# Narrow matrices on TensorE: where the transposes of maxima, the gate logits and V's scale matmul stand beside the P V bursts

## The chip, the cores and the metric

The kernel runs on one NeuronCore of a Trainium2 chip. The metric is the device time of one execution in microseconds (us). TensorE (PE) is shown in the profile as two rows: PE, the matmuls, and PEld, the loads of the stationary matrix that goes with each matmul. The other engines are VectorE (DVE), ScalarE (ACT), GpSimd (POOL) and SyncE (SP), which only issues DMAs here.

## The reference

An attention over 8 batches and 8 heads, and a mixture of experts behind it. Queries are averaged in pairs first, so that 576 pooled queries meet 1152 keys of 64 numbers each.

```python
q_pool = q.reshape(B, H, S // 2, 2, D).mean(axis=3)
scores = np.matmul(q_pool, k.transpose(0, 1, 3, 2)) / np.sqrt(D)
scores = scores - np.max(scores, axis=-1, keepdims=True)
attn = np.exp(scores)
attn = attn / (np.sum(attn, axis=-1, keepdims=True) + 1e-09)
attn_out = np.matmul(attn, v)
...
x = attn_out.transpose(0, 2, 1, 3).reshape(B * S, H * D)      # 4608 x 512
logits = x @ w_gate                                           # 8 experts
e_idx = np.argmax(logits, axis=1)
...
h = np.maximum(x[mask] @ w1[e], 0.0)
out[mask] = gate_w[mask, None] * eom[mask, e, None] * (h @ w2[e])
```

## The kernel before

**Stages.** First comes the attention, over 32 pairs of heads (8 batches of 4 pairs); it fills about the first two thirds of the span. Behind it stand the expert layers (`Moe.run`), which the change leaves alone. Nearly all matmuls of the attention are in one of two formats: fp32r (shown as f32 in the profile) for scores, maxima and logits, and f16 for P V.

**One step.** The attention runs in steps `s`, 18 for a pair, and the order on each engine is the order in which the Python loop emits (`manual_schedule`). One step emits on PE:

- the scores of one key chunk of one head, transposed (keys on partitions): two matmuls of L393 and two of L395, each with its own load of 128 columns, 288 columns wide. The exponentials on ACT (L399/L400 or L407/L408) follow, in two PSUM buffers that alternate;
- one chunk of row maxima in an even step and two in an odd one: two matmuls of L330 (384 columns wide), whose product DVE reduces to one maximum per query (L331). This runs 18 steps ahead of the scores that need it;
- in even steps only, a **P V burst** of the pair that is behind by `ALAG` = 6 steps: `BURST` says how many key chunks, mostly two. A chunk is 15 matmuls (L424, L425, L426) 64 or 65 columns wide, each with its own f16 load of 128 columns.

**The small work between.** Three kinds of small PE work stand among these, and they are what the change moves.

- *Transposes of maxima* (`rows`, L365): when the maxima of 4 or 5 query tiles are complete, the 128 x 4 or 128 x 5 tile `m` is transposed by a matmul whose stationary matrix is `m` itself (4 or 5 columns) and whose moving one is the identity, 128 columns wide. In the next step DVE splits the result in two parts `mr` (L370, L371), and in the step after that ACT issues two small DMAs (L125, `qb<-mr`) that put them as extra rows into `qb`, which the scores read. There are 64 of them; before the change 58 stood between L330 and a P V burst.
- *Gate logits* (`logits`, L496): when a pair's P V is normalised, its 128 columns of x are transposed (L479), split in high and low parts, and multiplied by the gate weights `wgt`: two matmuls, high and low, for 256 rows of x and two more for 320 rows. `wgt` has 32 columns that matter, padded with zeros to `WC` = 128. A generator yields 0 or 1 after each piece: the loop at `for r in routers` calls it at the head of a step, after a yield of 1 only in an even one. So the logits stood at the head of an even step, before its scores. There are 64 such pairs of matmuls.
- *V's scale* (`gmax`, L272): one fp32 matmul with a matrix of ones (128 columns loaded) and two columns moving; the profile shows it as two passes. The table `PREP` gives for each preparatory work of a pair the third of a step at which it is emitted: phase 0 is just behind the scores, phase 1 just behind the first chunk of maxima, phase 2 at the end of the step. `gmax` stood at 93, phase 0. There is one per pair.

`psum()` hands out three PSUM buffers in turn for L330, L365, L479, L496 and L272; some of these hold one until DVE has read it.

Of the kernel before, what the change touches and what calls it, by code (L numbers as in the profile page):

```python
# [26 lines left out]
         (45, 'sl', 0, 1), (46, 'sk', 1, 0), (48, 'sk', 1, 1), (51, 'sq1'), (54, 'sl', 1, 0), (57, 'sl', 1, 1), (56, 'lv'),  # L27
         (78, 'amax', 0), (82, 'amax', 1), (99, 'gmax'), (100, 'scale', 0), (100, 'scale', 1), (100, 'scale', 2), (103, 'vh', 0), (103, 'vs', 0), (106, 'vh', 1), (107, 'vl', 0), (109, 'vs', 1), (113, 'vl', 1))
PREP = ((0, 'lk'), (12, 'kh', 0), (12, 'qsum'), (17, 'kh', 1), (18, 'kl'), (18, 'dk', 0), (19, 'dk', 1), (22, 'qh'), (24, 'dq', 0), (25, 'dq', 1), (26, 'ql'), (29, 'qd'), (30, 'dl', 0), (32, 'dl', 1),
        (63, 'lv'), (82, 'amax', 0), (88, 'amax', 1), (93, 'gmax'), (94, 'scale', 0), (95, 'scale', 1), (99, 'scale', 2), (100, 'vh', 0), (101, 'vs', 0), (103, 'vl', 0), (107, 'vh', 1), (107, 'vs', 1), (110, 'vl', 1))  # L30
BURST = {0: 2, 2: 2, 4: 2, 6: 2, 8: 1, 10: 2, 12: 2, 14: 2, 16: 3}
PLP = (1, 3, 7, 9, 11, 13)
PLPL = (1, 3, 5, 17)
# [11 lines left out]
P32 = 6  # L45
SLEAD = 32
S = 1152
WC = 128
NQ = 576
NC = 9  # L50
SHIFT = 4.0 * math.log(2.0)
# [15 lines left out]
def attention(tc, qT, kT, vL, wg, keep, xrows, idscr, cum, pairs, setup, scat, init, exps):  # L67
    nc = tc.nc
    nb = len(pairs) // 4
    with ExitStack() as ctx:  # L70
# [16 lines left out]
        def psum(hold=False, name="tp"):  # L87

            while len(held) == 3:
                pop() if fill else pendv.pop(0)()  # L90
            k = next(i for i in banks if i not in held)
            free(k)
            if hold:
                held.add(k)
            x = ps_m.tile([128, 512], F32, name=name, tag=f"mp{k}")
            return (x, k) if hold else x

        def free(k):
            held.discard(k)
            banks.remove(k)  # L100
            banks.append(k)
# [22 lines left out]
        def dmaf(o, i, q=nc.sync):  # L124
            q.dma_start(out=o.bitcast(F32), in_=i.bitcast(F32))  # L125
# [220 lines left out]
        def pop(k=1):  # L346
            while k and fill:
                fill.pop(0)()
                k -= 1
# [3 lines left out]
        def sends():  # L353

            while pendd and pendd[0][1] < now[0]:
                pendd.pop(0)[0]()
# [3 lines left out]
        def rows(force=False):  # L360
            while pend_t and (force or now[0] >= pend_t[0][-1] + TLAG):
                m9, nt, t0, t1, qbf, _ = pend_t.pop(0)
                tp, tk = psum(True)
                tp = tp[0:nt, 0:128]
                nc.tensor.transpose(out=tp, in_=m9[:, 0:nt], identity=ident)  # L365
                mr = sm.tile([5, 2, 128], F32R, name="mr")[0:nt]
                c0 = 16.0 * SHIFT

                def split(tp=tp, tk=tk, mr=mr, qbf=qbf, t0=t0, t1=t1, nt=nt):
                    nc.vector.tensor_scalar(out=mr[:, 0], in0=tp, scalar1=c0, scalar2=None, op0=ALU.subtract)  # L370
                    nc.vector.scalar_tensor_tensor(out=mr[:, 1], in0=tp, scalar=c0, in1=mr.bitcast(F32)[:, 0], op0=ALU.subtract, op1=ALU.subtract)  # L371
                    free(tk)

                    def send():
                        for j in range(2):
                            dmaf(qbf[66 + j:67 + j, 128 * t0:128 * t1].rearrange("o (t n) -> o t n", n=128), mr[:, j], nc.scalar)
                    pendd.append((send, now[0]))
                if now[0] < 18:
                    split()
                else:  # L380
                    pendv.append(split)
# [60 lines left out]
        routers = []  # L442

        wf = bp.tile([128, 4, 16], F32, name="wf")
        wgt = bp.tile([128, 4, WC], F32R, name="wgt")
        em8 = keep['em8']
# [23 lines left out]
        def logits(b, c, xb):  # L470

            xh = sm.tile([128, NQ], F32R, name="xh", bufs=1)
            xl = sm.tile([128, NQ], F32R, name="xl", bufs=1)
            yield 1
            for c0, c1, grp in ((0, 256, (0, 1)), (256, NQ, (2, 3, 4))):
                tx, tk = psum(True)
                for i, t in enumerate(grp):
                    x = xb[:, t, 128 * c:128 * c + 128]
                    nc.tensor.transpose(out=tx[:, 128 * i:128 * i + 128], in_=x, identity=ident)  # L479
                d = 0  # L480
                for o, w in ((0, c1 - c0),) if c0 == 0 else ((0, 256), (320, 64)):
                    z = slice(c0 + d, c0 + d + w)
                    nc.scalar.copy(out=xh[:, z], in_=tx[:, o:o + w])

                    def sub(o=o, w=w, z=z, tx=tx, tk=tk if not d else None):
                        nc.vector.tensor_tensor(out=xl[:, z], in0=tx[:, o:o + w], in1=xh.bitcast(F32)[:, z], op=ALU.subtract)
                        if tk is not None:
                            free(tk)
                    fill.insert(0, sub)
                    d += w  # L490
                yield 1
            for c0, c1 in ((0, 256), (256, NQ)):
                pop(99)
                tl = psum()
                for j, x in enumerate((xh, xl)):
                    nc.tensor.matmul(tl[:, 0:c1 - c0], lhsT=wgt[:, c], rhs=x[:, c0:c1], start=j == 0, stop=j == 1)  # L496
                if c == 0:
                    nc.vector.tensor_copy(out=lT[:, c0:c1], in_=tl[0:32, 0:c1 - c0])
                else:
                    nc.vector.tensor_tensor(out=lT[:, c0:c1], in0=tl[0:32, 0:c1 - c0], in1=lT[:, c0:c1], op=ALU.add)  # L500
                yield 1
            if c == 3:
                yield from router(b, xb)

# [117 lines left out]
        def adv(k, g, want):  # L622
            while pos[k] < want:
                next(g, None)
                pos[k] += 1
# [3 lines left out]
        def prep_at(s, ph):  # L629
            u = 3 * (s + SLEAD) + ph  # L630
            for n in range(max(u // 54 - 2, 0), min(u // 54 + 2, NP)):
                r = u - 54 * n + min(3 * (LEAD - 15), 2 * n)
                if r == 0:
                    preps[n] = prep(n, PREP if n > 1 else PREP0 if n else PREPF)
                if n in preps:
                    for f in preps[n].pop(r, ()):
                        f()

        E = mybir.EngineType
        with tc.manual_schedule(engines={E.PE, E.DVE, E.Activation, E.Pool}):  # L640
            for s in range(-SLEAD, 0):
                for ph in range(3):
                    prep_at(s, ph)
                if s == -RI:
                    for i in (1, 2):
                        dmaf(QBs[i][64:66], QBs[0][64:66])
                        dmaf(KBs[i][64:68], KBs[0][64:68])
                if s == 1 - SLEAD + INIT:
                    consts()
                if s == -3:  # L650
                    init(0)
                if s >= -int(L0):
                    adv('m', mg, int(1.5 * (s + 1 + L0)))
                    now[0] = s
                    sends()
                    pop(3)
                    rows()
            for s in range(18 * NP + 14):
                now[0] = s
                live = s < 18 * NP  # L660
                if s % 18 == 2 and 0 < s // 18 < 5:
                    with tc.issue_after(lastk[0].ins):
                        init(s // 18)
                sends()
                while pendv:
                    pendv.pop(0)()
                for r in routers:
                    if not s % 2 or not live or not r[1]:
                        r[1] = next(r[0], 0)
                pop()  # L670
                if live:
                    next(sg)
                prep_at(s, 0)
                mw = min(27 * NP, int(1.5 * (s + 1 + min(LEAD, L0 + LS * s))))
                if pos['m'] < mw:
                    adv('m', mg, pos['m'] + 1)
                prep_at(s, 1)
                adv('m', mg, mw)
                if s < 54 or s % 2 == 0:
                    rows()  # L680
                if pos['m'] == 27 * NP:
                    pop(2)
                j = s - ALAG
                for _ in range(BURST.get(j % 18, 0) if 0 <= j < 18 * NP else 0):
                    next(ag)
                prep_at(s, 2)
                if not live:
                    pop(3)
            pop(99)
            for r in routers:  # L690
                for _ in r[0]: pass
# [513 lines left out]
```

## Time and profile before

| | before |
|---|---|
| time, median of 3 runs | 1521.67 us (1519.01 to 1526.12) |
| the profiled execution's own time | 1524.1 us |
| its span | 1522.4 us |
| PE busy, share of the span | 1477.5 us, 97% |
| PEld busy | 1339.5 us, 88% |
| DVE, ACT, POOL busy | 72%, 74%, 66% |
| granted TensorE clock, mean | 0.995 |

A row of the timeline reads: start in us from the span's start, duration in us, engine, line, operation, tiles (written <- read), shapes, and how many such instructions in a row were merged. Matmuls overlap in a pipeline, so the duration of one says little; what one costs is read from the distance between starts. Starts are shown to 0.01 us, and a distance worked out from two of them is good to about that much. A row of the groups reads: line, engine, operation, tiles, shapes, count, then busy time in us, mean duration of one in ns, and the idle time before it with what ended it.

### The profile page before, as it was taken

The page shows a single profiled execution, that of the slowest core. Times are in us where ns is not written, and L with a number is a line of the kernel's source. Part 1 is how long each engine was busy: PE and PEld are TensorE (multiplying, and loading weights), DVE is VectorE, ACT ScalarE, POOL GpSimd, SP SyncE. Part 2 cuts the span into 40 slices and gives each one's busy share as a digit, 9 for nine tenths or more (in the row PEclk, how much of TensorE's full clock was granted, in tenths as well). Part 3 has the DMA queues.
Part 4 walks back from the last instruction along what each step waited for, and adds up shares of the span by engine and source line. Part 5 has one row for each costly group of instructions (what it writes and reads, how often), then busy time and mean ns, then how long its engine had stood idle before and what let it go on. Part 6 is the DMA issues. An engine that isn't in the chain of part 4 may idle for free. (4 is left out here: it accounts for less than half of the span.)

```text
span 1522.4 us, 40889 instructions
## 1 busy us (share of the span) xinstructions
PE 1477.5 (97%) x15838; PEld 1339.5 (88%) x15838; DVE 1103.0 (72%) x2336; ACT 1122.4 (74%) x1949; POOL 1010.2 (66%) x892
## 2 busy tenths in 40 slices
PE   7999999999999999999999999979999999999997
PEld 6899999999999999999999899967888888888875
DVE  7677777777786777777777777747777777777862
ACT  5888888888888888888888788875565565565542
POOL 5887898788878889788878988786333333333200
PEclk9999999999999999999999999989999999999999
DMA  5577566665676566646666567165736666645451
GB/s 169 142 184 186 134 159 169 169 151 134 156 172 160 135 153 163 173 121 164 165 163 161 142 157 172 35 251 174 303 106 227 234 222 217 213 143 172 165 190 50
DMA packets 91984, 253.35 MB, mean 166 GB/s; under 512 B 12714, under 2 KB 16954, under 8 KB 91778
## 3 DMA queue, kind: packets, MB, share of 16 engines
q1 hardware_dynamic: 81194, 228.93, 54.4%
q0 software_dynamic: 9152, 20.85, 3.9%
q8 instruction: 129, 2.11, 0.6%
q10 hardware_dynamic: 1440, 0.89, 0.2%
q14 instruction: 69, 0.57, 0.1%
HBM read 164.23 MB, written 23.02 MB: 123 GB/s over the span
## 5 line engine op out<-in xcount | busy, mean ns | idle before, releaser
L331 DVE TENSOR_REDUCE pm<-mp 128x1 f32<-128x384 f32 x864 | 451.7, 549 | 213.3 <-PE mp L330 212.5
L409 POOL TENSOR_TENSOR pl<-p,ph 128x576 f16<-128x576 f32 x386 | 494.2, 1286 | 146.3 <-ACT ph L408 104.4
L407 ACT ACTIVATE p<-sps 128x576 f32<-128x576 f32 x386 | 252.8, 655 | 97.7 <-PE sps L395 56.4
L330 PE MATMUL mp<-ka,qa 128*128 128x384 f32 x960 | 314.1, 343 | 0.0
L424 PEld LDWEIGHTS <-ph 128*128 128x128 f16 x2880 | 262.0, 96 | 39.3 <-issue 30.0
L424 PE MATMUL av<-vt,ph 128*128 128x65 f16 x2880 | 294.4, 194 | 0.0
L425 PE MATMUL av<-vt,ph 128*128 128x64 f16 x2880 | 292.4, 194 | 0.0
L426 PE MATMUL av<-vt,pl 128*128 128x65 f16 x2880 | 291.5, 192 | 0.0
L393 PE MATMUL sps<-qa,ka 128*128 128x288 f32 x1152 | 277.3, 322 | 12.6 <-ACT ph L408 7.2
L425 PEld LDWEIGHTS <-ph 128*128 128x128 f16 x2880 | 264.9, 97 | 0.8
L426 PEld LDWEIGHTS <-pl 128*128 128x128 f16 x2880 | 265.1, 99 | 0.0
L330 PE MATMUL mp<-kb,qb 66*128 66x384 f32 x768 | 260.2, 339 | 1.2 <-DVE kb L204 0.6
L408 ACT ACTIVATE ph<-sps 128x576 f16<-128x576 f32 x386 | 251.6, 652 | 0.0
L395 PE MATMUL sps<-qb,kb 68*128 68x288 f32 x1152 | 246.3, 296 | 0.0
L906 PE MATMUL hps<-x,w1h 128*128 128x512 f32 (+1 forms) x704 | 231.7, 390 | 7.1 <-DVE x L890 4.2
L393 PEld LDWEIGHTS sps<-qa,ka 128*128 128x128 f32 x1152 | 182.8, 190 | 17.9 <-ACT ph L408 10.8
L395 PEld LDWEIGHTS sps<-qb,kb 68*128 68x128 f32 x1152 | 185.0, 189 | 0.0
L330 PEld LDWEIGHTS mp<-ka,qa 128*128 128x128 f32 x960 | 178.1, 190 | 1.7 <-DVE pm L331 1.5
L908 ACT COPY hs<-hps 128x512 f32<-128x512 f32 (+1 forms) x88 | 49.0, 557 | 171.9 <-PE hps L906 166.4
L906 PE MATMUL hps<-x,w1l 128*128 128x256 f32 (+1 forms) x704 | 166.1, 277 | 0.0
L403 DVE TENSOR_TENSOR pl<-sps,ph 128x576 f16<-128x576 f32 x190 | 143.5, 755 | 17.8 <-ACT sps L400 14.8
L399 ACT ACTIVATE ph<-sps 128x576 f16<-128x576 f32 x190 | 124.4, 655 | 39.9 <-PE sps L395 30.8
(231 smaller groups left out, 2942.1 us busy)
## 6 DMA issues: line engine op xcount, KB each, us to landing
ka<-xk SPq DMA_DIRECT2D x120, 288.0 KB
raw1b<-in_w_dram SPq DMA_DIRECT2D x24, 1024.0 KB
raw2b<-in_w_dram SPq DMA_DIRECT2D x24, 1024.0 KB
raw1a<-in_w_dram SPq DMA_DIRECT2D x22, 1024.0 KB
raw2a<-in_w_dram SPq DMA_DIRECT2D x22, 1024.0 KB
vp<-in_vL_dram SPq DMA_DIRECT2D x32, 576.0 KB
qp<-in_qT_dram SPq DMA_DIRECT2D x31, 576.0 KB
kpf<-in_kT_dram SPq DMA_DIRECT2D x31, 576.0 KB
```

The costliest lines, as they stand in the source:

```text
L330: nc.tensor.matmul(mp, lhsT=l, rhs=r, start=j == 0, stop=j == len(ops) - 1)
L331: nc.vector.tensor_reduce(out=pm[:, i:i + 1], in_=mp, axis=AX.X, op=ALU.max)
L393: nc.tensor.matmul(sps[:, j, 0:288], lhsT=ka[:, h, ks], rhs=qa[:, o + 288 * j:o + 288 * j + 288], start=True, stop=False)
L395: nc.tensor.matmul(sps[:, j, 0:288], lhsT=kb[:, h, ks], rhs=qb[:, h, 288 * j:288 * j + 288], start=False, stop=True)
L403: nc.vector.tensor_tensor(out=pl.rearrange("p (j n) -> p j n", j=2), in0=x, in1=ph2, op=ALU.subtract)
L407: nc.scalar.activation(out=p32.rearrange("p (j n) -> p j n", j=2), in_=x, func=AF.Exp, scale=1.0 / 16)
L408: e_ = nc.scalar.activation(out=ph2, in_=x, func=AF.Exp, scale=1.0 / 16)
L409: nc.gpsimd.tensor_tensor(out=pl, in0=p32, in1=ph, op=ALU.subtract)
L424: nc.tensor.matmul(av_[:, qb, 0:65], lhsT=hi, rhs=vt[:, h, c, 0:65], start=c == 0 and qb == 0, stop=False)
L425: nc.tensor.matmul(av_[:, qb, 0:64], lhsT=hi, rhs=vt[:, h, c, 66:130], start=False, stop=False)
L426: nc.tensor.matmul(av_[:, qb, 0:65], lhsT=lo, rhs=vt[:, h, c, 0:65], start=False, stop=c == NC - 1 and qb == 4)
L906: nc.tensor.matmul(hp[:, f, 0:n], lhsT=W1[l][g][:, c, fs], rhs=d['x'][:, c, 0:n], start=c == 0 and l == 0, stop=c == 3 and l == 0)
```

## The change

The weights of the gate get 32 columns in place of 128, and their product 32 partitions. The logits' pieces now yield 2 where they are to be called just behind the next P V burst of an even step, and the loop does that call; the first pair of logit matmuls comes behind the burst of the step in which the second group of transposes was made, the second pair two even steps later. `rows` runs behind the burst in even steps (before step 54 in its old place too). `gmax` goes from phase 0 to phase 1, which in an even step is directly ahead of the burst, and the first two pieces of DVE work on its result one phase later each.

```diff
-        (63, 'lv'), (82, 'amax', 0), (88, 'amax', 1), (93, 'gmax'), (94, 'scale', 0), (95, 'scale', 1), (99, 'scale', 2), ...
+        (63, 'lv'), (82, 'amax', 0), (88, 'amax', 1), (94, 'gmax'), (95, 'scale', 0), (96, 'scale', 1), (99, 'scale', 2), ...
...
-WC = 128
+WC = 32
...
                     d += w
-                yield 1
+                yield 1 if c0 == 0 else 2
             for c0, c1 in ((0, 256), (256, NQ)):
                 pop(99)
                 tl = psum()
                 for j, x in enumerate((xh, xl)):
-                    nc.tensor.matmul(tl[:, 0:c1 - c0], lhsT=wgt[:, c], rhs=x[:, c0:c1], start=j == 0, stop=j == 1)
+                    nc.tensor.matmul(tl[0:32, 0:c1 - c0], lhsT=wgt[:, c], rhs=x[:, c0:c1], start=j == 0, stop=j == 1)
...
-                yield 1
+                if c0 == 0:
+                    yield 2
+                yield 2 if c0 == 0 else 1
...
                 for r in routers:
-                    if not s % 2 or not live or not r[1]:
+                    if not live or not r[1] or r[1] == 1 and not s % 2:
                         r[1] = next(r[0], 0)
...
-                if s < 54 or s % 2 == 0:
+                if s < 54:
                     rows()
                 if pos['m'] == 27 * NP:
                     pop(2)
                 j = s - ALAG
                 for _ in range(BURST.get(j % 18, 0) if 0 <= j < 18 * NP else 0):
                     next(ag)
+                if s % 2 == 0:
+                    rows()
+                    for r in routers:
+                        if r[1] == 2:
+                            r[1] = next(r[0], 0)
```

What stands on PE around V's scale matmul, in the program before: the end of an odd step, a whole even step with the second pair of logits at its head, and the first matmul of its burst (`tp` is a PSUM buffer of `psum()`, `am` the maxima of V, `mp` a chunk of maxima, `sps` scores, `av` the P V product).

```order
L330 MATMUL mp_4952<-ka_122,qa_125 128x384
L330 MATMUL mp_4952<-kb_119,qb_128 128x384
L496 MATMUL tp<-xh,wgt 128x320
L496 MATMUL tp<-xl,wgt 128x320
L393 MATMUL sps_4965<-qa_124,ka_121 128x288 x2
L395 MATMUL sps_4965<-qb_127,kb_118 128x288 x2
L272 MATMUL tp<-am,onesf 128x2
L330 MATMUL mp_4976<-ka_122,qa_125 128x384
L330 MATMUL mp_4976<-kb_119,qb_128 128x384
L424 LDWEIGHTS ph
L424 MATMUL av_4669<-vt_138,ph 128x65
```

The same even step on PE in the changed program, from the end of the odd step before it:

```order
L330 MATMUL mp_4952<-ka_122,qa_125 128x384
L330 MATMUL mp_4952<-kb_119,qb_128 128x384
L393 MATMUL sps_4961<-qa_124,ka_121 128x288 x2
L395 MATMUL sps_4961<-qb_127,kb_118 128x288 x2
L330 MATMUL mp_4970<-ka_122,qa_125 128x384
L330 MATMUL mp_4970<-kb_119,qb_128 128x384
L272 MATMUL tp<-am,onesf 128x2
L424 LDWEIGHTS ph
L424 MATMUL av_4669<-vt_138,ph 128x65
```

Here `gmax` stands between the maxima and the burst, and the logits are gone from the head of the step. They stand at the end of that burst in the changed program, again on PE:

```order
L426 LDWEIGHTS pl
L426 MATMUL av_4669<-vt_138,pl 128x65
L496 MATMUL tp<-xh,wgt 32x320
L496 MATMUL tp<-xl,wgt 32x320
L393 MATMUL sps_5002<-qa_124,ka_121 128x288 x2
L395 MATMUL sps_5002<-qb_127,kb_118 128x288 x2
```

The logits now lie between the last f16 matmul of the burst and the scores of the next step. A transpose of maxima stands in the same way in the changed program, one even step earlier:

```order
L426 LDWEIGHTS pl
L426 MATMUL av_4669<-vt_138,pl 128x65
L365 MATMUL tp<-ident,m_4799 5x128
L393 MATMUL sps_4941<-qa_124,ka_121 128x288 x2
L395 MATMUL sps_4941<-qb_127,kb_118 128x288 x2
```

It stood between L330 and the first L424 of that burst before. Over the whole program 57 of the 64 transposes of maxima now stand between a burst and scores, and 61 of the 64 pairs of logit matmuls; of the 32 scale matmuls 28 stand directly ahead of a burst, where 2 stood before. The other instructions keep their order on PE.

More of the change, by code (lines that the diff above doesn't have):

```diff
@@ L29 @@
 PREP = ((0, 'lk'), (12, 'kh', 0), (12, 'qsum'), (17, 'kh', 1), (18, 'kl'), (18, 'dk', 0), (19, 'dk', 1), (22, 'qh'), (24, 'dq', 0), (25, 'dq', 1), (26, 'ql'), (29, 'qd'), (30, 'dl', 0), (32, 'dl', 1),
-        (63, 'lv'), (82, 'amax', 0), (88, 'amax', 1), (93, 'gmax'), (94, 'scale', 0), (95, 'scale', 1), (99, 'scale', 2), (100, 'vh', 0), (101, 'vs', 0), (103, 'vl', 0), (107, 'vh', 1), (107, 'vs', 1), (110, 'vl', 1))
+        (63, 'lv'), (82, 'amax', 0), (88, 'amax', 1), (94, 'gmax'), (95, 'scale', 0), (96, 'scale', 1), (99, 'scale', 2), (100, 'vh', 0), (101, 'vs', 0), (103, 'vl', 0), (107, 'vh', 1), (107, 'vs', 1), (110, 'vl', 1))
 BURST = {0: 2, 2: 2, 4: 2, 6: 2, 8: 1, 10: 2, 12: 2, 14: 2, 16: 3}
```

## The prediction

> **What bounds the kernel now.** I first read busy time by stretches, to see whether TensorE carries the attention; one batch (four pairs) takes about 124 us there. The columns are the stretch and its length, then busy us (and instructions) of PE, PEld, DVE, ACT and POOL, the granted clock, DMA share and GB/s.
>
> ```profile
> 472.00:596.00 124.00, 122.16 (x1669) 115.45 (x1666) 92.27 (x234) 104.98 (x195) 104.89 (x92) 1.00 0.63 155
> ```
>
> PE is busy 122.2 of 124 us, ACT 105, POOL 105, DVE 92. Second, the waits of PE: the largest that an engine of the steady attention ends is this one (total us, times, longest).
>
> ```profile
> PE sps L393 <- ACT ph L408: 7.2, 9, 1.1
> ```
>
> So ACT holds PE up nine times by about 0.8 us; the rest of the attention is a queue of PE work without gaps. Time taken out of that queue should come off the end, unless one of those nine waits swallows it. As busy time says nothing about what one matmul costs, I read the distances between starts in the timeline of PE. First the ordinary neighbours: the end of a burst, the step behind it, and the start of the next burst.
>
> ```profile
> 500.31 0.19 PE L426 MATMUL av<-vt,pl 128*128 128x65 f16 x1
> 500.34 0.51 PE L393 MATMUL sps<-qa,ka 128*128 128x288 f32 x2
> 500.68 0.43 PE L395 MATMUL sps<-qb,kb 68*128 68x288 f32 x2
> ...
> 501.48 0.34 PE L330 MATMUL mp<-kb,qb 66*128 66x384 f32 x1
> 501.66 0.43 PE L393 MATMUL sps<-qa,ka 128*128 128x288 f32 x2
> 501.92 0.43 PE L395 MATMUL sps<-qb,kb 68*128 68x288 f32 x2
> ...
> 502.36 0.33 PE L330 MATMUL mp<-kb,qb 66*128 66x384 f32 x1
> 502.54 0.20 PE L424 MATMUL av<-vt,ph 128*128 128x65 f16 x1
> ```
>
> The two L393 take 0.34 us behind a burst (500.34 to 500.68) and 0.26 behind L330 (501.66 to 501.92). The burst costs the scores 0.08 us: a wide f32 load doesn't fit under a P V matmul, of which one starts each 0.03 us. Keep three distances: L426 to L395, 0.37 us; L330 to L395, 0.44; L330 to L424, 0.18. What a small piece of work costs is the distance with it, less the one without it.
>
> **Part 1, transposes of maxima.** Ahead of a burst, as before:
>
> ```profile
> 495.58 0.33 PE L330 MATMUL mp<-kb,qb 66*128 66x384 f32 x1
> 495.75 0.27 PE L365 MATMUL tp<-ident,m 128*4 128x128 f32 x1
> 495.86 0.19 PE L424 MATMUL av<-vt,ph 128*128 128x65 f16 x1
> ```
>
> L330 to L424 is 0.28 us, so one costs 0.10. The trace has none between a burst and scores, but a few of the first steps stand directly ahead of scores; here are the matmuls, then the load of those scores:
>
> ```profile
> 93.36 0.33 PE L330 MATMUL mp<-kb,qb 66*128 66x384 f32 x1
> 93.53 0.27 PE L365 MATMUL tp<-ident,m 128*4 128x128 f32 x1
> 93.56 0.51 PE L393 MATMUL sps<-qa,ka 128*128 128x288 f32 x2
> 93.91 0.43 PE L395 MATMUL sps<-qb,kb 68*128 68x288 f32 x2
> ```
>
> ```profile
> 93.53 0.30 PEld L393 LDWEIGHTS sps<-qa,ka 128*128 128x128 f32 x2
> ```
>
> The load of L393 starts together with L365 (93.53), so the transpose and the first wide load run side by side: L365 to L395 is 0.38 us. Behind a burst I expect 0.03 from L426 to L365, then those 0.38: 0.41 in place of 0.37, a cost of 0.04 us. The load that burst and scores expose anyway is spent under the transpose. Saved: 0.10 - 0.04 = 0.06 us, 57 times, **3.4 us**. The bounds: 0.10 - 0.11 if the overlap fails (below nothing: -0.6 us; 0.11 is what it costs ahead of scores behind L330, 93.36 to 93.91 less 0.44), and 0.10 each, 5.7 us, if it comes free. I take the row that shows the overlap.
>
> What else hangs on L365: it now runs behind the burst's 30 matmuls, about 0.9 us later. DVE's split waits for it, ACT's DMA for the split, and in ACT's queue the next exponentials stand behind that DMA. For the L365 of 495.75:
>
> ```profile
> 496.80 0.27 DVE L370 TENSOR_SCALAR mr<-tp 4x128 fp32r<-4x128 f32 x1
> ```
>
> ```profile
> 497.64 0.60 ACTq L125 DMA_DIRECT2D qb<-mr  x1
> ```
>
> The burst begins 0.10 us earlier than at 495.86 and lasts 0.9, so L365 would run from 496.7 and end at 497.0 (0.27 us); the split starts 0.2 us later than at 496.80 and its first half is done by 497.3, still 0.3 us before ACT issues its DMA. On DVE the next reduction waits for maxima behind the next scores, which PE does after L365. So nothing is held up here; if that cover were gone, ACT and then the scores would wait up to 0.2 us, 62 times.
>
> **Part 2, logits.** Before, at the head of a step:
>
> ```profile
> 419.03 0.34 PE L330 MATMUL mp<-kb,qb 66*128 66x384 f32 x1
> 419.21 0.28 PE L496 MATMUL tp<-xh,wgt 128*128 128x256 f32 x1
> 419.33 0.28 PE L496 MATMUL tp<-xl,wgt 128*128 128x256 f32 x1
> 419.44 0.43 PE L393 MATMUL sps<-qa,ka 128*128 128x288 f32 x2
> 419.71 0.43 PE L395 MATMUL sps<-qb,kb 68*128 68x288 f32 x2
> ```
>
> L330 to L395 is 0.68 us, a cost of 0.24 over the 0.44. The scores lose nothing to their load behind a logit matmul (419.44 to 419.71, 0.27 us, as behind L330). Behind a burst: 0.03, then the 0.50 from 419.21 to 419.71, is 0.53 in place of 0.37, a cost of 0.16. Saved 0.08, provided that the load of `wgt` itself fits under the last P V matmul. With 128 columns it would not, by the 0.08 us that scores lose there, and nothing would be saved. The trace has no f32 load of 32 columns; its nearest rows, with 5 and with 128, are these (mean ns behind the second bar's busy us):
>
> ```profile
> L365 PEld LDWEIGHTS tp<-ident,m 128*5 128x5 f32 x32 | 2.8, 87 | 1.0 <-DVE m L338 0.6 <-DVE ri L785 0.4
> L393 PEld LDWEIGHTS sps<-qa,ka 128*128 128x128 f32 x1152 | 182.8, 190 | 17.9 <-ACT ph L408 10.8 <-DVE pl L403 1.9 <-issue 1.8
> ```
>
> On a straight line between 87 and 190 ns, 32 columns take 110 (an estimate), about a fifth of the way; a fifth of the exposed 0.08 us is 0.02, and I take 0.01, since part of it overlaps the burst's last matmul. Saved 0.07 us, 61 times, **4.3 us**; bounds 0 (it loads like 128 columns) and 4.9 (0.08, nothing exposed). The 320-column pairs have the same loads and wider matmuls, so I give them the same saving. [...]
>
> **Part 3, V's scale.** Before, between scores and maxima:
>
> ```profile
> 454.85 0.44 PE L395 MATMUL sps<-qb,kb 68*128 68x288 f32 x2
> 455.12 0.28 PE L272 MATMUL tp<-am,onesf 128*128 128x2 f32 x2
> ...
> 455.71 0.20 PE L424 MATMUL av<-vt,ph 128*128 128x65 f16 x1
> ```
>
> L395 to L424 is 0.86 us; without it, in the first fence, 0.62 (501.92 to 502.54). It costs 0.24, as its two columns hide neither its second load nor that of L330. Two of them stand ahead of a burst already:
>
> ```profile
> 145.60 0.34 PE L330 MATMUL mp<-kb,qb 66*128 66x384 f32 x1
> 145.78 0.28 PE L272 MATMUL tp<-am,onesf 128*128 128x2 f32 x2
> 145.92 0.19 PE L424 MATMUL av<-vt,ph 128*128 128x65 f16 x1
> ```
>
> L330 to L424 is 0.32 us, a cost of 0.14, because the f16 load behind it is short. Saved 0.10 us, 28 times, **2.8 us**, bounds 2.2 and 3.4 for the reading of the starts. Who waits for `gmax` is DVE two thirds of a step later, and V is needed steps after that.
>
> **The sum.** 3.4 + 4.3 + 2.8 = 10.5 us. Against it stand the nine waits for ACT. ACT falls behind over a few steps, PE runs up to it, and what PE saves within such a stretch lengthens the wait. At most one of each kind lies there, 0.06 + 0.07 + 0.10 = 0.23 us, or 2.1 us over nine; I take half, 1 us. The expert phase is untouched. So 9.5 us come off: the profiled execution would go from 1524.1 to 1514.6, and the median of the runs, 2.4 below it, from 1521.7 to **1512.2**; I say 1512. With the bounds of the parts the forecast's own range is 1508 to 1516: 5.7 + 4.9 + 3.4 = 14.0 off at the best, and 6 off where the narrow load exposes half of 0.08 us and the waits take 2.
>
> **Rivals.**
>
> *ACT takes over the saving.* ACT is busy 105 of 124 us, and its issues of `qb<-mr` (sixteen in a batch, 0.60 us each) bring it to about 115; POOL too has 105. If half of the 10.5 us turns into longer waits at L393, 5 us remain: 1516.5. For it: the nine waits are there already, once or so in each batch. Against it: 115 is still below the 122.8 us that a batch would then take (124 less an eighth of 9.5).
>
> *The loads do not overlap narrow matmuls behind a burst.* Then a wide load waits until the narrow matmul before it is through, transposes cost 0.11 in place of 0.10, logits 0.24 as before, and only V's scale gains: 2.8 - 0.6 = 2.2 us off, 1519.5. Against it speaks the load that starts with L365 at 93.53. [...]
>
> *Narrow matrices drain the array, and the kernel gets slower.* The trace has matmuls that use a part of the array, the transposes of logits over 32 rows:
>
> ```profile
> 672.89 0.33 PE L330 MATMUL mp<-kb,qb 66*128 66x384 f32 x1
> 673.16 0.49 PE L521 MATMUL tp<-ident,lT 32*128 32x32 f32 x5
> 673.58 0.53 PE L393 MATMUL sps<-qa,ka 128*128 128x288 f32 x2
> 673.94 0.42 PE L395 MATMUL sps<-qb,kb 68*128 68x288 f32 x2
> ```
>
> L330 to L521 is 0.27 us in place of 0.18, and the scores behind it take 0.36 in place of 0.26: 0.09 to enter and 0.10 to leave. If 32 columns act like 32 rows, each pair of logits pays these 0.19 and the scores' load as well, 0.08: 0.27 us 61 times, 16.5 us, and the time is 1512.2 + 16.5 = 1528.7, slower than before. From 0.16 us a pair on, the kernel loses. Against it: the 4 and 5 columns of L365 are narrower still, and enter at 495.75, 0.17 us behind L330.
>
> That the change does not do what it says is excluded by the order on PE above.
>
> **How the numbers follow.** Forecast 0.68, ACT takes half 0.16, no overlap 0.08, drained array 0.06, something else with no change 0.02. About 0.5% (7.6 us, or 1514.1) is what a measurement of this kernel can tell from no change. Of the forecast's 0.68 some 0.60 lie below 1514.1. The rest, with ACT's 0.16, the 0.08 and the 0.02, and half of the drained case, is within: 0.36. Slower by over 0.5% (above 1529.3) is left with 0.04. The range reaches from 1507 to 1518; it takes in the forecast and ACT's case, 0.84, less the edges, and leaves the other two out.
>
> **What would show it.** In the changed trace L426 to L365 to L393 should read 0.03 and 0.03 with L395 0.38 behind L365; L496 should follow L426 within 0.03 to 0.05 us, with L395 0.50 (256 columns) behind it, and its load should be near 110 ns; L330 to L424 around L272 should be 0.32. A batch should take 1.2 us less. It is wrong if L496's load stays near 190 ns, if L365 to L395 or the last L496 to L395 is 0.08 us longer than in the rows above, or if the wait for ACT at L393 grows from 7.2 us by more than 2.

## The result, and the profile after

| | before | after |
|---|---|---|
| time, median of 6 runs each | 1522.63 us (1519.01 to 1532.02) | 1533.05 us (1530.02 to 1539.84) |
| ratio, 95% interval | | 1.0057 (1.0035 to 1.0079) |
| the profiled execution's own time | 1524.1 us | 1530.0 us |
| its span | 1522.4 us | 1528.2 us |
| last P V matmul starts at | 1014.4 us | 1021.8 us |
| granted TensorE clock (the share of full speed that TensorE is given), mean | 0.995 | 0.995 |

The changed kernel is slower, by 0.6% by the ratio (the quotient of the two medians is 1.0068). The profile puts the loss into the attention: its last P V matmul comes 7.4 us later, and what follows takes 506.4 us in place of 508.0.

First the stretch of the steady attention, in the same columns as before:

```profile
472.00:596.00 124.00, 121.35 (x1659) 113.36 (x1658) 93.56 (x233) 104.61 (x194) 104.54 (x92) 1.00 0.63 155
```

In the same 124 us PE runs 1659 matmuls in place of 1669. It is not that each of them got dearer: PE is busy for less, 121.35 in place of 122.16 us. There are gaps. The waits of PE say which; ahead stands the engine that waited, then tile and line of what was late, then total us, times, longest:

```profile
PE mp L330 <- DVE lT L500: 10.9, 22, 0.5
...
PE sps L393 <- ACT ph L408: 5.3, 8, 2.1
...
PE mp L330 <- DVE lT L498: 3.5, 7, 0.5
```

The wait for ACT became shorter (7.2 to 5.3 us); the scores' other wait, for the subtraction on DVE (L403), grew from 5.0 to 6.3. Two rows are new: matmuls of maxima (L330) that wait for DVE's work on the logits (L500 adds a product to `lT`, L498 copies it for the first pair of a batch), 29 times, 14.4 us. Here is one, in the timeline of PE: V's scale ahead of a burst, the second pair of logits behind it, and the step that follows.

```profile
489.72 0.34 PE L330 MATMUL mp<-kb,qb 66*128 66x384 f32 x1
489.90 0.28 PE L272 MATMUL tp<-am,onesf 128*128 128x2 f32 x2
490.04 0.19 PE L424 MATMUL av<-vt,ph 128*128 128x65 f16 x1
...
490.47 0.19 PE L426 MATMUL av<-vt,pl 128*128 128x65 f16 x1
490.50 0.31 PE L496 MATMUL tp<-xh,wgt 128*32 128x320 f32 x1
490.65 0.31 PE L496 MATMUL tp<-xl,wgt 128*32 128x320 f32 x1
490.80 0.44 PE L393 MATMUL sps<-qa,ka 128*128 128x288 f32 x2
491.07 0.43 PE L395 MATMUL sps<-qb,kb 68*128 68x288 f32 x2
491.34 0.34 PE L330 MATMUL mp<-ka,qa 128*128 128x384 f32 x1
491.52 0.34 PE L330 MATMUL mp<-kb,qb 66*128 66x384 f32 x1
492.36 0.44 PE L330 MATMUL mp<-ka,qa 128*128 128x384 f32 x1 [0.49 <-DVE lT L500]
```

The distances around the moved work are those of the forecast: L330 to L424 around L272 is 0.32 us, L426 to L496 is 0.03, and from there 0.57 to L395 (320 rows; 0.56 before the change, so the forecast's "same saving" holds). The gap is further on. The second chunk of maxima starts 0.84 us behind the matmul before it (491.52 to 492.36), where 0.18 is usual: 0.66 us lost, of which the profile calls 0.49 a wait for L500. DVE at the same place:

```profile
490.49 0.55 DVE L331 TENSOR_REDUCE pm<-mp 128x1 f32<-128x384 f32 x1
490.95 0.22 DVE L433 TENSOR_SCALAR r<-av,sc 128x5 f32<-128x5 f32 x1
491.20 0.19 DVE L434 RECIPROCAL r<-r 128x5 f32<-128x5 f32 x1
491.42 0.49 DVE L435 TENSOR_TENSOR xb<-av,r 128x320 f32<-128x320 f32 x1
491.83 0.47 DVE L500 TENSOR_TENSOR lT<-tp,lT 32x320 f32<-32x320 f32 x1
...
492.41 0.16 DVE L279 TENSOR_SCALAR inv<-tp 128x2 f32<-128x2 f32 x1
```

The logits are done on PE at 490.96 (490.65 and 0.31), but L500, which frees their PSUM buffer, runs only from 491.83: the three instructions of `norm` (L433 to L435, 0.88 us from 490.95 to 491.83) stand ahead of it. Before the change, DVE did the same work in this order, the add ahead of everything:

```profile
485.89 0.47 DVE L500 TENSOR_TENSOR lT<-tp,lT 32x320 f32<-32x320 f32 x1
...
486.93 0.16 DVE L279 TENSOR_SCALAR inv<-tp 128x2 f32<-128x2 f32 x1
487.01 0.21 DVE L433 TENSOR_SCALAR r<-av,sc 128x5 f32<-128x5 f32 x1
```

**The theory.** `norm`, which divides a finished P V product by its sums, lies in the list `fill`, and `logits` empties that list with `pop(99)` (L493) before it asks for a buffer. At the head of a step there was nothing of weight in it. Behind a burst there is: in the step of the second pair of logits the first head of the next pair has just ended its P V, and its `norm` has just been queued. So `pop(99)` now puts 0.88 us of DVE work ahead of the logits' add. At that moment V's scale holds another of the three buffers of `psum()` (from L272 until L279 is through, at 492.57). The first chunk of maxima takes the third, and the second chunk is handed the logits' buffer, which comes next in turn, and has to wait until L500 ends. By this theory it takes both: the add behind `norm`, and the buffer held by `gmax`.

The sum of the attention, from all distances between starts of PE in the two profiled executions (a distance more than 0.06 us above the median for its two neighbours is counted as a wait, by its excess): ordinary work of PE 9.4 us less, waits 15.4 us more (29.4 to 44.8), and 1.5 us more in stretches of half clock (granted clock 0.50). That is 7.5 us more from PE's first matmul to the last of P V (1006.9 to 1014.4 us). The new wait alone is 29 × 0.66 = 19.1 us; other waits fell by some 4 us. So the saving was there, and a wait of twice its size came with it.

The rival theories: the buffer held across so many steps is enough by itself; the loss is spread over the three parts; or the narrow matrix itself is what costs.

### The profile page after: what moved, and what is told of

It reads as the page before. It is cut to its first block, busy times and chain, and to the rows that moved or that the text cites. A ratio compares the mean times of both kernels' runs of the same rounds, so it can differ in the third digit from the quotient of the medians.

```text
span 1528.2 us, 40889 instructions
## 1 busy us (share of the span) xinstructions
PE 1472.4 (96%) x15838; PEld 1325.1 (87%) x15838; DVE 1115.7 (73%) x2336; ACT 1122.6 (73%) x1949; POOL 1010.5 (66%) x892
## 5 line engine op out<-in xcount | busy, mean ns | idle before, releaser
L330 PE MATMUL mp<-ka,qa 128*128 128x384 f32 x960 | 314.8, 344 | 14.4 <-DVE lT L500 10.9
L424 PEld LDWEIGHTS <-ph 128*128 128x128 f16 x2880 | 263.6, 97 | 40.0 <-issue 35.7
L424 PE MATMUL av<-vt,ph 128*128 128x65 f16 x2880 | 295.3, 194 | 0.0
L426 PE MATMUL av<-vt,pl 128*128 128x65 f16 x2880 | 292.0, 192 | 0.0
L393 PE MATMUL sps<-qa,ka 128*128 128x288 f32 x1152 | 273.1, 318 | 11.8 <-DVE pl L403 6.3
L426 PEld LDWEIGHTS <-pl 128*128 128x128 f16 x2880 | 265.4, 99 | 0.0
L330 PE MATMUL mp<-kb,qb 66*128 66x384 f32 x768 | 259.6, 338 | 0.9 <-DVE kb L204 0.6
L395 PE MATMUL sps<-qb,kb 68*128 68x288 f32 x1152 | 246.5, 296 | 0.0
L393 PEld LDWEIGHTS sps<-qa,ka 128*128 128x128 f32 x1152 | 186.2, 190 | 20.0 <-ACT ph L408 8.7
L330 PEld LDWEIGHTS mp<-ka,qa 128*128 128x128 f32 x960 | 177.7, 189 | 25.2 <-DVE lT L500 17.8
L395 PEld LDWEIGHTS sps<-qb,kb 68*128 68x128 f32 x1152 | 185.4, 189 | 0.2 <-issue 0.2
L403 DVE TENSOR_TENSOR pl<-sps,ph 128x576 f16<-128x576 f32 x190 | 143.6, 756 | 17.3 <-ACT sps L400 16.1
```

Of the source, the lines that this page charges most:

```text
L330: nc.tensor.matmul(mp, lhsT=l, rhs=r, start=j == 0, stop=j == len(ops) - 1)
L393: nc.tensor.matmul(sps[:, j, 0:288], lhsT=ka[:, h, ks], rhs=qa[:, o + 288 * j:o + 288 * j + 288], start=True, stop=False)
L395: nc.tensor.matmul(sps[:, j, 0:288], lhsT=kb[:, h, ks], rhs=qb[:, h, 288 * j:288 * j + 288], start=False, stop=True)
L403: nc.vector.tensor_tensor(out=pl.rearrange("p (j n) -> p j n", j=2), in0=x, in1=ph2, op=ALU.subtract)
L424: nc.tensor.matmul(av_[:, qb, 0:65], lhsT=hi, rhs=vt[:, h, c, 0:65], start=c == 0 and qb == 0, stop=False)
L426: nc.tensor.matmul(av_[:, qb, 0:65], lhsT=lo, rhs=vt[:, h, c, 0:65], start=False, stop=c == NC - 1 and qb == 4)
```

## Experiments

Each kernel is compared with runs of the kernel before on the same chip: medians 1524.3 us for the first four, 1525.18 for the next four, 1525.34 for the last two.

### Norm behind the logits

The changed kernel, but the second pair of logits doesn't empty the list:

```diff
-                pop(99)
+                if c0 == 0:
+                    pop(99)
```

> The changed kernel, but the second pair of logit matmuls no longer empties the list of waiting DVE work first, so the normalisation of the pair's first head (three DVE operations, about 0.9 us) stands behind the logits' add on DVE and not ahead of it. Theory N (the add waits behind the normalisation, and the next maxima wait for the add's PSUM buffer, 29 times some 0.66 us): the wait of L330 for the add goes, the time falls by about 19 us from 1533, to 1512 to 1516, below the kernel before. Rival D (DVE has too much to do in this step in whatever order): the wait moves to another reader of PSUM, PE still loses at least 0.3 us each time, 1522 to 1530. Rival B (only two PSUM buffers are left while V's scale holds the third): the wait at L330 shrinks by the normalisation's share only if the add is then done before the second chunk of maxima; if it is not, over 8 us of waiting stay.

Measured: 1522.15 us (1517.55 to 1528.24, 12 runs), ratio 0.9992 (0.9974 to 1.0011). DVE at the place in question (L501 is the add here, as the edit adds a line):

```profile
521.37 0.55 DVE L331 TENSOR_REDUCE pm<-mp 128x1 f32<-128x384 f32 x1
521.88 0.48 DVE L501 TENSOR_TENSOR lT<-tp,lT 32x320 f32<-32x320 f32 x1
...
522.35 0.20 DVE L433 TENSOR_SCALAR r<-av,sc 128x5 f32<-128x5 f32 x1
```

PE there, the chunks of maxima of the odd step:

```profile
522.39 0.34 PE L330 MATMUL mp<-kb,qb 66*128 66x384 f32 x1
522.57 0.34 PE L330 MATMUL mp<-ka,qa 128*128 128x384 f32 x1
```

The add is ahead of `norm` again, the second chunk starts 0.18 us behind the first, and of the 29 waits of L330 for the logits one is left (1.6 us). 11 us come back (1533.05 to 1522.15). But the time is that of the kernel before, 6 to 10 us above what was expected without the wait. The waits of PE show part of what is left:

```profile
PE sps L393 <- ACT ph L408: 8.5, 6, 2.6
...
PE tp L524 <- DVE inv L279: 2.5, 7, 0.4
```

The second row is new: at the end of a batch the router's transposes (L524 here) find no buffer, since V's scale holds one until L279.

### Scale earlier, norm still ahead

The changed kernel, with V's scale two thirds of a step earlier, so that its buffer is free again by then:

```diff
-(94, 'gmax'), (95, 'scale', 0), (96, 'scale', 1)
+(92, 'gmax'), (93, 'scale', 0), (94, 'scale', 1)
```

> The changed kernel, but V's scale matmul at the end of the odd step before, so that its PSUM buffer is free again when the logits take theirs; the normalisation stays ahead of the add. Rival B: with three buffers in turn the second chunk of maxima no longer gets the logits' buffer; the wait of L330 for the add goes, and what is lost again is the scale's saving (2.8 us): 1516 to 1519. Theory N alone (the place of the normalisation is enough): the wait stays, 14 us by the waits, and the time is 1533 + 3 = 1534 to 1537. If both are needed, this one and the one with the normalisation behind the add both lose the wait. Rival D: the wait turns up at another line, 1525 to 1535.

Measured: 1525.11 us (1520.06 to 1531.95), ratio 1.0021 (1.0004 to 1.0039). Its waits of L330 for the logits:

```profile
PE mp L330 <- DVE lT L500: 1.0, 2, 0.5
PE mp L330 <- DVE lT L498: 0.4, 1, 0.4
```

DVE still does the end of `norm` directly ahead of the add:

```profile
485.94 0.49 DVE L435 TENSOR_TENSOR xb<-av,r 128x320 f32<-128x320 f32 x1
486.35 0.47 DVE L500 TENSOR_TENSOR lT<-tp,lT 32x320 f32<-32x320 f32 x1
```

`norm` is ahead as in the changed kernel, and still only 3 of the 29 waits are left. So `norm` alone makes no such wait; it needs the buffer that V's scale holds. Both halves of the theory are shown by taking away either. The time, though, is 3 us above that of the experiment before and 6 above the 1516 to 1519 that were expected without the wait. The profiled execution was the fastest of the twelve (1520.06 us), so its trace doesn't tell where those 6 us went.

### Logits earlier

The changed kernel, with the second pair of logits two steps earlier, away from `norm` and from V's scale:

```diff
-                if c0 == 0:
-                    yield 2
                 yield 2 if c0 == 0 else 1
```

> The changed kernel, but the second pair of logit matmuls comes one even step earlier, behind a transpose of maxima in the same place; no normalisation is waiting there, and it is the transpose that holds a PSUM buffer. Theory N: no normalisation, no wait; 28 pairs share the exposed load with a transpose, so 28 x 0.08 = 2 us of the saving go: 1514 to 1518. Rival B (a held buffer suffices): the wait of L330 for the add stays near 14 us, the time near 1533.

Measured: 1544.2 us (1540.64 to 1549.61, 6 runs), ratio 1.014 (1.0113 to 1.0168); neither expectation holds.

```profile
PE sps L393 <- ACT ph L408: 12.3, 8, 3.2
PE sps L393 <- DVE xl L486: 7.9, 5, 2.2
...
PE mp L330 <- DVE inv L279: 4.3, 7, 0.6
```

The wait of L330 for the logits is gone, so a held buffer by itself does not make it. Other waits take its place. The second row is put down to L486, the split of x, which scores do not read; DVE does it right behind L403, which the scores do wait for, and in the longest case (2.1 us) L403 itself had waited 2.96 us for ACT. In the third row the maxima wait for V's scale to give back its buffer; by the code the router, which begins two steps earlier too, holds another, but that was not tested. These three rows give 24.5 us, 17.3 more than the wait for ACT before the change; the time is some 20 above the kernel before, and the mean granted clock of the runs is lower too (0.9875 over 6 runs, against 0.9930 over 29).

### The gate's matrix wide again

The kernel of the first experiment with 128 columns, to measure what the narrow load is worth:

```diff
-WC = 32
+WC = 128
...
-tl[0:32, 0:c1 - c0]
+tl[:, 0:c1 - c0]
```

> As the kernel with the normalisation behind the add, but with gate weights of 128 columns as before. If a narrow load fits under the last P V matmul and a wide one doesn't (as the distances of the trace have it), the first logit matmul behind a burst starts its partner 0.08 us later, 61 times 0.08 = 4.9 us over the kernel with 32 columns: near 1518. If the width does not matter behind a burst, the two are equal.

Measured: 1525.43 us (1520.79 to 1532.79), ratio 1.0013 (0.9995 to 1.0032), 3.3 us above the first experiment, in place of the 4.9 expected; the two intervals overlap, so the distances on PE have to show it. PE behind a burst:

```profile
513.47 0.36 PE L497 MATMUL tp<-xh,wgt 128*128 128x256 f32 x1
513.67 0.28 PE L497 MATMUL tp<-xl,wgt 128*128 128x256 f32 x1
```

From the first to the second L497 it takes 0.20 us (median 0.201 for 256 rows, against 0.123 in the narrow form; 0.230 against 0.151 for 320): 0.078 us × 61 = 4.8 us, the 0.08 that the prediction took for a wide load. The narrow matrix is not what costs, and moving wide logits behind bursts would have saved next to nothing on PE.

### The three parts alone

The maxima's transposes behind the burst, in the kernel before:

```diff
-                if s < 54 or s % 2 == 0:
+                if s < 54:
                     rows()
...
+                if s % 2 == 0:
+                    rows()
```

> The kernel before with the transposes of maxima alone moved behind the bursts. The prediction's part 1: 57 times 0.06, 3.4 us below the kernel before, no new wait. If the later split held up ACT's DMAs, the waits of L393 for ACT would grow from 7.2 us and the time would not fall.

Measured: 1523.58 us (1519.05 to 1529.58), ratio 0.9992 (0.9974 to 1.001), by the medians 1.6 us less. The wait of L393 for ACT is 7.9 us here, against 7.2 and 6.8 in the two profiles of the kernel before.

V's scale alone, in the kernel before:

```diff
-(93, 'gmax'), (94, 'scale', 0), (95, 'scale', 1)
+(94, 'gmax'), (95, 'scale', 0), (96, 'scale', 1)
```

> The kernel before with V's scale matmul alone moved directly ahead of the burst. The prediction's part 3: 28 times 0.10, 2.8 us below the kernel before.

Measured: 1524.64 us (1519.88 to 1531.94), ratio 0.9992 (0.9972 to 1.0011), 0.5 us less. One of its waits:

```profile
PE tp L521 <- DVE inv L279: 1.5, 7, 0.2
```

The router's wait for L279 belongs to this part: held one phase longer, the buffer is missing when the router starts. From the last L330 to L521 PE takes 0.548 us seven times, against 0.265: 2.0 of the 2.8 us that this part was to save.

Logits alone (32 columns, behind bursts; the edit is of the changed kernel and puts transposes and scale back):

```diff
-(94, 'gmax'), (95, 'scale', 0), (96, 'scale', 1)
+(93, 'gmax'), (94, 'scale', 0), (95, 'scale', 1)
...
-                if s < 54:
+                if s < 54 or s % 2 == 0:
                     rows()
...
                 if s % 2 == 0:
-                    rows()
                     for r in routers:
```

> The kernel before with the logits alone moved behind the bursts, in 32 columns, with the normalisation pulled ahead of the add as in the change; V's scale in its old place holds a PSUM buffer here too. Theory N: this part alone carries the loss, 29 waits of L330 for the add at 0.66 us less 61 times 0.07 saved: 19 - 4 = 15 us over the kernel before, near 1538. Rival B2 (it takes the new place of V's scale as well): no such wait, 4 us below the kernel before.

Measured: 1539.93 us (1536.47 to 1541.97, 6 runs), ratio 1.0091 (1.0065 to 1.0117), 14.8 us more.

```profile
PE mp L330 <- DVE lT L500: 11.8, 22, 1.6
...
PE mp L330 <- DVE lT L498: 4.3, 7, 1.0
```

The 29 waits belong to this part, with V's scale in its old place, which holds its buffer at that time too: in 29 of the 32 places L279 comes behind the add. The parts add up to −1.6 − 0.5 + 14.8 = 12.7 us, against 10.4 between the medians of the whole change.

### All three parts, without both waits

The kernel of the first experiment, and L279 a phase earlier, so that the buffer is free for the router:

```diff
-(94, 'gmax'), (95, 'scale', 0), (96, 'scale', 1)
+(94, 'gmax'), (95, 'scale', 0), (95, 'scale', 1)
```

> As the kernel with the normalisation behind the add, and the second piece of DVE work on V's scale follows at once on the first, ahead of the normalisation, so that the scale's PSUM buffer is free 0.9 us earlier. In the kernel with the normalisation behind the add, the transposes of logits waited for that buffer, 7 times some 0.4 us (2.5 us by the waits). Theory N: that wait goes, nothing else changes, 2.5 to 3 us less than that kernel: 1517 to 1520, and about 4 us below the kernel before. Rival D (DVE has too much to do here): the wait moves to another line, no gain.

Measured: 1521.15 us (1516.46 to 1527.25), ratio 0.9975 (0.9956 to 0.9994): faster than the kernel before by 4 us, and than the changed one by some 12. Neither the wait for the logits nor the router's is left; these two are the largest of the steady attention:

```profile
PE sps L393 <- ACT ph L408: 8.1, 9, 1.7
...
PE sps L393 <- DVE pl L403: 6.1, 9, 1.5
```

It is the best of all versions, and by the medians still gives less than half of the 10.5 us. The next two runs ask where the rest went.

### The maxima's DMAs on another queue

In the changed kernel ACT sits at its issue of a pair of the maxima's DMAs (ACTq is its queue) for 3.3 us, with the DMA engines at 0.95 of their time (the last section has the window):

```profile
362.91 3.34 ACTq L125 DMA_DIRECT2D qb<-mr  x2
```

Here, in the kernel just shown, SP issues them:

```diff
-mr[:, j], nc.scalar)
+mr[:, j], nc.sync)
```

> As the kernel with the scale's buffer freed early, but the two small DMAs that put the maxima into qb are issued by SP and no longer by ACT. In the traces ACT stands idle 2 to 3 us once in a batch at these issues, L393 waits for ACT there (8 us in all), and drops of the granted clock follow the longest of these waits. Theory A (the rest of the saving is lost to ACT's issues and the clock drops behind them): the wait of L393 for ACT falls below 3 us, no drop of the clock in the middle of the attention, 6 to 10 us less: 1511 to 1515. If SP's own queue is in the way (its loads stand behind the split of the maxima), the scores wait for ka, kb or qb instead, and the time does not fall or rises.

Measured: 1527.12 us (1522.41 to 1531.96), ratio 1.0005 (0.9989 to 1.0022), slower than with ACT's queue.

```profile
PE sps L395 <- DMA qb<-mr: 18.1, 14, 3.3
```

PE's wait for ACT is nearly gone (0.3 us, once), but the scores now wait for the maxima's rows themselves, 14 times. For the wait that ends at 619.38, here is the split on DVE, the last load ahead of the rows in SP's queue, the rows, and the scores:

```profile
609.32 0.28 DVE L371 SCALAR_TENSOR_TENSOR mr<-tp,mr 5x128 fp32r<-5x128 f32 x1
614.84 0.46 SPq L125 DMA_DIRECT2D kb<-kp  x1
615.61 1.59 SPq L125 DMA_DIRECT2D qb<-mr  x2
619.38 0.52 PE L395 MATMUL sps<-qb,kb 68*128 68x288 f32 x2 [2.79 <-DMA qb<-mr]
```

SP issues these rows 6.0 us after the split was done, behind other loads (1.0 to 6.0 us over the 14), and they reach the scores 2.2 us after that (1.8 to 5.1). So SP's queue is in the way, as the second half of the expectation had it. What ACT's queue costs is not decided by this run, and the theory that the rest is lost there stays open.

### The kernel before, once more

> The kernel before unchanged, for a second profile: whether its attention runs without drops of the granted clock, as in the first profile (1014 us to the last P V matmul, no drop before it). If drops belong to the waits at ACT's issues that this kernel has as well, some appear here too.

Measured: 1518.14 us (a single run), a span of 1516.4, the last P V matmul at 1009.7, and no drop of the clock ahead of it, as in the first profile; the attention of this unchanged kernel is 3.7 us shorter than in its first profile (1003.2 against 1006.9 us, from the first matmul of PE to that one). A single profile is good to some 4 us. Against this one, the attention of the version without both waits (1000.8 us) has 8 us less of ordinary PE work, 2 us more of waits, and 3 us more in stretches of half clock. Those 3 us are of one execution: the mean clock of the runs that the two versions were compared by is 0.9913 (12 runs) and 0.9920 (29 runs of the kernel before), and 0.0007 of the span is 1 us (an estimate). With clocks down to 0.988 in these 29, and 0.995 in both its profiles, the clock of the kernel before must have been lowered for longer in other executions.

## Why the prediction was wrong

**Part 1, transposes.** The place costs what was forecast. PE after the change:

```profile
360.09 0.19 PE L426 MATMUL av<-vt,pl 128*128 128x65 f16 x1
360.12 0.27 PE L365 MATMUL tp<-ident,m 128*5 128x128 f32 x1
360.15 0.51 PE L393 MATMUL sps<-qa,ka 128*128 128x288 f32 x2
360.50 0.43 PE L395 MATMUL sps<-qb,kb 68*128 68x288 f32 x2
```

0.03, 0.03 and 0.35: 0.41 from L426 to L395, as worked out; the medians over the run are the same. Alone, the part gave 1.6 of the 3.4 us, with an interval (0.9974 to 1.001, so −4.0 to +1.5 us) that holds the 3.4 as well; "nothing is held up" is neither shown nor refuted by it.

**Part 2, logits: the step that failed.** On PE it was right: 0.03 from L426 to L496, 0.50 from there to L395 (the medians for 256 rows are 0.026 + 0.122 + 0.118, and 0.264 for the two L393), and the load of 32 columns takes what the straight line gave:

```profile
L496 PEld LDWEIGHTS tp<-xl,wgt 128*32 128x32 f32 x64 | 7.0, 110 | 0.7 <-DVE xl L486 0.7
```

But the part was costed as a place on PE alone. The prediction followed DVE and ACT behind L365, and never behind L496: not the `pop(99)` that runs with the logits, not the add that frees their buffer, nor who else holds a buffer then. A term of 29 × 0.66 = 19.1 us is missing from the sum, and the part came out at 14.8 us lost in place of 4.3 gained; the 29 distances in the trace add up to 19.0. The order of the changed program on DVE has it, from the end of one step to the middle of the next:

```
L403 TENSOR_TENSOR pl<-sps_10461,ph 128x576
L331 TENSOR_REDUCE pm<-mp_10490 128x1
L433 TENSOR_SCALAR r<-av_10189,sc 128x5
L434 RECIPROCAL r<-r 128x5
L435 TENSOR_TENSOR xb<-av_10189,r 128x5x64
L500 TENSOR_TENSOR lT<-tp,lT 32x320
L277 TENSOR_SCALAR tp<-tp 128x2
L279 TENSOR_SCALAR inv_9287<-tp 128x2
```

L433 to L435 ahead of L500, and L279, with which V's scale gives its buffer back, behind it: both halves of the wait stand there, and the prediction gave the order of PE only.

**Part 3, V's scale.** 0.32 us around L272 as forecast. "Who waits for `gmax` is DVE two thirds of a step later" named who needs the value and not who needs the buffer: the router does, seven times, 2.0 us of the 2.8.

**The waits for ACT** were to swallow 1 us. After the change they shrank (7.2 to 5.3 us), since PE lost time elsewhere; in the version without both new waits they are 8.1 us, 0.9 us over before, which is the size that was taken. But the prediction counted one row: the scores' wait for L403, which works on ACT's exponentials, went from 5.0 to 6.1 us beside it, so the two together took 2.0.

**The rivals.** ACT didn't take over: without the new waits these two rows took 2 us of the 10.5, where the rival needed 5. That loads don't overlap, and that narrow matrices drain the array, are both refuted by the distances, 0.03 us into L365 and L496 and 0.12 from the last L496 of 256 rows to the scores. The rival on the slow side was a mechanism of the array, and the 0.04 for slower rested on it alone; the one that came is a wait for a buffer, of which no case spoke. None of the three marks by which the prediction was to be called wrong came: they were a load, two distances on PE and the old wait for ACT, and none could show a new wait. The batch, which was to take 1.2 us less, took 0.9 more (7.5 over eight).

**What stays open.** Without the new waits the three parts give 4.0 us (by the interval 0.9 to 6.7), where the sum said 9.5. Ordinary PE work fell by 8 us there and by 9.4 in the changed kernel, so the 10.5 us of the parts are right within 1 to 2.5; the rest went into waits and half-clock stretches (2 and 3 us in the one pair of profiles; by the clocks of all runs the stretches are 1 us). Why the waits grow is not shown.

## What to carry to other kernels

A step that is moved takes along everything its code calls: the work that it flushes onto other engines and the buffer that it holds until they have run it. Before pricing the new place on the engine that it leaves and enters, read the order on the engine that must free its buffer, and count who holds the other buffers that are handed out in turn at that moment. Where a saving per place is 0.07 us and a missed buffer costs 0.66, one miss in ten eats the gain.

## What the runs showed of the hardware

*A load of 32 columns beside one of 128, behind a burst.* Behind an f16 burst the load of 32 columns (110 ns, against 190 for 128) costs next to nothing: 0.026 us from L426 to L496, and 0.123 from there to the second L496 (256 rows), where it was 0.119 with the wide load at the head of a step before the change. The wide load behind a burst makes these 0.123 us 0.201, 0.078 more.

*Behind 10 of 12 long idle stretches of PE the granted clock fell.* The windows of the changed kernel around the issue at 362.91 that held ACT for 3.3 us (stretch and length, busy us of PE, PEld, DVE, ACT, POOL, clock, DMA share, GB/s):

```profile
363.00:369.00 6.00, 3.36 (x32) 2.48 (x29) 3.26 (x12) 2.70 (x6) 1.55 (x3) 0.98 0.95 207
368.80:372.20 3.40, 3.40 (x35) 3.40 (x32) 0.70 (x2) 2.30 (x5) 3.24 (x4) 0.50 0.70 215
```

The same stretch before the change:

```profile
363.00:369.00 6.00, 5.00 (x61) 4.54 (x58) 3.59 (x12) 4.76 (x9) 3.52 (x3) 1.00 0.98 211
```

The DMA share is as high before (0.98), but PE idles 1.0 us in that stretch, and 2.6 after; only after does the clock fall to 0.50, for 3.4 us, which costs 1.7 us of full speed. Over all twelve profiles, from 60 us to the last P V matmul, a drop began within 5.5 us of the start of 10 of the 12 idle stretches of PE above 1.9 us, and of 8 of the 20 between 1.2 and 1.9. The two profiles of the kernel before, with one such stretch (1.33 us), have no drop there. In the changed kernel the idle time ahead of the drop is in pieces: of the 6.00 us of the window that ends at 369.00 PE was busy for 3.36, and its longest wait, for ACT, was 2.1 us. What sets a drop off is not shown.
